# Two more pairs in the seven-product form, three decodings moved two stages on, two pieces of products moved

## The chip, the cores and the metric

The kernel runs on one core of one Trainium2 chip. The metric is device time in microseconds (us) of the whole kernel, as the median of the runs made. A profile of one execution comes with it: for every engine (TensorE = PE, VectorE = DVE, ScalarE = ACT, GpSimd = POOL, SyncE = SP, which issues the DMAs) it has the start and the duration of each instruction.

## The reference, cut to what matters

Linear attention with a decay, then a mixture of four experts, then one more gated network; all in fp32.

```python
x = retention(q, k, v, lam)              # 2 x 768 tokens, 8 heads of 64: x is 1536 x 512
p = domain_probs / (domain_probs.sum(-1, keepdims=True) + 1e-9)
out = 0
for e in range(4):                       # moe_w1: 4 x 512 x 1024, moe_w2: 4 x 1024 x 512
    out += p[:, e:e+1] * (relu(x @ w1[e]) @ w2[e])
h = out @ w_in                           # moe2_w_in: 512 x 2048
g = h * (1 / (1 + exp(-h)))
return g @ w_out                         # moe2_w_out: 2048 x 512
```

The two weights of the last network, moe2_w_in and moe2_w_out, come to the chip as 64-bit numbers and are brought to fp32 there.

## The kernel before, in words

The 1536 tokens are three groups of 512. Every fp32 product is made of three matmuls on fp32r halves: high x high, low x high, high x low. A high half is a copy by ACT, a low half a subtraction after it by DVE or POOL (`split`, lines 145 to 150).

There are four stages, one after the other on PE.

- **Stage a** (36 steps of `gemm1` and `gemm2`): attention for all tokens, and the experts for the first 512 tokens.
- **Stage c**: the experts for the other 1024 tokens. Each of 16 pairs `i` multiplies a 512 x 256 block of w1 by 1024 tokens in seven products instead of eight (`LEFT`, `product`, six matmuls each) and then multiplies the result by w2. Pairs 0 to 7 (`pair_step`) do that second multiplication plainly, as 8 pieces of 6 matmuls (`down`, line 803). Pairs 8 to 15 (`pair7`) do it by seven products for two pairs at a time, as 14 pieces of 6 matmuls (`down7`, line 981). `SW = NW // 2` is the first pair of the second kind.
- **Stage b**: the last network for the first 512 tokens, 16 steps of `gemm1` (12 matmuls, line 553) and, two steps later, `gemm2` (12 matmuls, line 609).
- **Stage d**: the last network for the other 1024 tokens, 8 pairs in `pair7`.

The order of the instructions on each engine is written out by hand. Between two products of a pair, `filler()` takes the next waiting piece from the list `fill`; `plan_n`, the last argument of `pair7`, says how many pieces come after each of the seven products. Each piece ends with an addition to the sum, put off to the next unit (`after`, `due`). In `pair7` the first product goes to a PSUM bank x, ACT copies x to y (line 1049), the second goes to z, and the third and fourth add to y, so that the third waits for the copy. After the fourth DVE makes v = y + s; from v, z, x and y come the gated values and their halves, in a chain over DVE and ACT.

In stage b, step `i` brings one 512 x 256 block of w_in in every second step: `left_sums` (four POOL sums, line 690) and `split_up` (one ACT copy, one POOL subtraction of 128x1024) for the block that PE uses two steps later. In the odd steps `split_down` does the same for w_out, and DMAs write three things for stage d to DRAM: the sums (`left_out`) and both halves of the block (`left_kept`). `combine` gives a list `mixing` of 11 jobs (differences on DVE, halves on ACT and DVE) that prepare the tokens for stage d; from step 3 on each step does one. Where a job has a second part, it is put in `pending` and is sent out at the start of the next step (`flush`).

A decoding (`decode`, 32 of them) takes 128x512 words of 64 bits to fp32: one ACT operation (line 200) and, after the next `flush`, four DVE operations (lines 207, 210, 213, 217; the last is the addition). `decode_next` stores the result of the decoding before, loads the words of a coming one and starts one. 18 of them are in stage a, 14 in pairs 0 to 6 of stage c.

Of the kernel before, what the change touches and what calls it, by code (L numbers as in the profile page):

```python
# [7 lines left out]
F32 = mybir.dt.float32  # L8
# [15 lines left out]
NF = 8  # L24
CW = B * P
TW = 512
HW = DM // 2
DECODE = 4
GI = 32
NN = 4  # L30
NW = E * NF // 2
NV = NF
SW = NW // 2


A12, A22, A21, A11 = range(4)
# [3 lines left out]
def kernel(  # L40
# [10 lines left out]
    nc = tc.nc  # L51
# [178 lines left out]
    def flush():  # L230
        while pending:
            pending.pop(0)()
# [475 lines left out]

    def left_kept(i):
        for n, t in enumerate(up_t["b", i]):  # L710
            nc.sync.dma_start(out=wu[i][:, n], in_=t[:, :4].bitcast(F32))

    def left_in(i):
        t = tmp["d"].tile([P, 4, HW], F32, tag="us", name="us")
# [435 lines left out]
    with tc.manual_schedule():  # L1150
# [75 lines left out]
        for i in range(NN, na):  # L1226
# [24 lines left out]
                load_gate("c", 0, 1)  # L1251
            if i == DECODE:
                start_decoder()
            elif DECODE < i < 4 * NF - NN and (i % 2 and i not in (5, 13) or i in (6, 14, 16, 18, 20, 22, 24, 26)):
                decode_next(i < 4 * NF - NN - 2)

            if i == NN:
                w_tiles(wp, ("a", 3))
# [19 lines left out]
                    job()  # L1278

        flush()  # L1280
        early.close()
        words.close()
        xa.close()
# [16 lines left out]
        for i in range(NW):  # L1300
# [29 lines left out]
                    jc.setdefault(gap, []).extend(lambda q=q: down_left(q) for q in qs)  # L1330
            if i == NW - 1:
                jc[4] = [lambda: split_up(("b", 0), False)]
            pair7(i - SW, jc, {SW: [1] * 7, SW + 1: [0, 1, 1, 1, 1, 1, 2]}.get(i))

        for _ in range(3):
            filler()
# [16 lines left out]
        for i in range(nb):  # L1353
            flush()
            gemm1("b", i)
            unit()
            if i < 2:
                for _ in range(3):
                    filler()
            elif i < nb - 2:  # L1360
                gemm2("b", i - 2)
            if i % 2:
                load(0)
                left_out(i // 2)
                for n in ([0, 1] if i == 1 else [i // 2 + 1]):
                    if n < NV:
                        left_kept(n)
                if i == nb - 3:
                    grp_t[("d", 0), 0] = hi, lo = up_tiles(wp)
                    split(nc.gpsimd, hi[:, 0], lo[:, 0], lead[0])  # L1370
                    split(nc.gpsimd, hi[:, 1:], lo[:, 1:], lead[1])
                if i < nb - 1:
                    split_down(("b", (i + 1) // 2))
                else:
                    fill += last_down("b", nb)
            else:
                left_sums(("b", i // 2))
                if i == nb - 2:
                    left_in2(0)
                if 2 <= i < nb - 2:  # L1380
                    split_up(("b", i // 2 + 1), False)
                if i == nb - 6:
                    lead = [
                        leftp.tile([P, 2 * DM], F32, tag="uc", name="lead")[:, :HW],
                        tmp["sums"].tile([P, 4, HW], F32, tag="lead", name="lead"),
                    ]
                    nc.sync.dma_start(out=lead[0], in_=wd[0][0][:, A11 * HW:])
                    nc.sync.dma_start(out=lead[1], in_=wu[0][:, 2])
            if i == 1:
                assert not fill  # L1390
                ops.close()
                tmp["sums"] = pool(sums, "sums2", side="right")
            if i == 2:
                mixing = combine(acc_t["c", 0], acc_t["c", 1])
            elif i > 2:
                for job in mixing[i - 3:i - 2]:
                    job()
        flush()
        sums.close()
        late.close()  # L1400
        tmp["d"] = tmp["s"] = tmp["op"] = pool(ctx, "dp", side="right")
# [2 lines left out]
        for i in range(NV):  # L1404
# [14 lines left out]
                plan.append((0, lambda: down_sums(i)))  # L1419
            for gap, fn in plan:  # L1420
                jobs.setdefault(gap, []).append(fn)
            pair7(i, jobs, {0: [0, 1, 1, 0, 1, 1, 1], 1: [0, 0, 1, 0, 0, 1, 2]}.get(i))
        for n, when in ((4, 0), (3, 0), (2, 3), (1, 5)):
            after(when, lambda n=n: down_left(7 * NV // 2 - n))
        fill[-1:] = [
# [61 lines left out]
```

## The time and the profile before

| what | value |
|---|---|
| median of 3 runs | 786.24 us (785.4 to 786.46) |
| the profiled execution's own time | 786.24 us |
| its span, from the first to the last instruction | 784.5 us |
| PE busy | 777.6 us, 99% of the span |
| DVE, ACT, POOL busy | 558.4, 370.3, 496.8 us |
| granted clock of TensorE | 1.00 of full speed all through |

The span is what the profile can explain; 1.7 us lie around it. Starts are in us from the start of the span. Busy time of PE includes the time in which a matmul's end is still on its way through the array, so that a busy PE can still lose time between the starts of two matmuls.

### The profile page before, as it was taken

The page shows a single profiled execution, that of the slowest core. Times are in us where ns is not written, and L with a number is a line of the kernel's source. Part 1 is how long each engine was busy: PE and PEld are TensorE (multiplying, and loading weights), DVE is VectorE, ACT ScalarE, POOL GpSimd, SP SyncE. Part 2 cuts the span into 40 slices and gives each one's busy share as a digit, 9 for nine tenths or more (in the row PEclk, how much of TensorE's full clock was granted, in tenths as well). Part 3 has the DMA queues.
Part 4 walks back from the last instruction along what each step waited for, and adds up shares of the span by engine and source line. Part 5 has one row for each costly group of instructions (what it writes and reads, how often), then busy time and mean ns, then how long its engine had stood idle before and what let it go on. Part 6 is the DMA issues. An engine that isn't in the chain of part 4 may idle for free.

```text
span 784.5 us, 11076 instructions
## 1 busy us (share of the span) xinstructions
PE 777.6 (99%) x4038; PEld 644.4 (82%) x4038; DVE 558.4 (71%) x812; ACT 370.3 (47%) x664; POOL 496.8 (63%) x458
## 2 busy tenths in 40 slices
PE   9999999999999999999999999999999999999998
PEld 8888888888888888888788888888888778888886
DVE  7345587786687588888778777784555577777775
ACT  3333434343455334433464646463445476666651
POOL 3856565443765455556698888877688855665642
PEclk9999999999999999999999999999999999999999
DMA  7877768553244334433102120215767525232302
GB/s 295 309 244 241 224 205 301 185 189 120 95 141 141 113 130 162 134 108 115 46 28 81 54 82 28 80 42 201 279 225 260 195 68 180 78 131 77 112 1 108
DMA packets 39913, 113.89 MB, mean 145 GB/s; under 512 B 4482, under 2 KB 6706, under 8 KB 39858
## 3 DMA queue, kind: packets, MB, share of 16 engines
q1 hardware_dynamic: 39856, 113.18, 42.6%
q8 instruction: 32, 0.52, 0.3%
q14 instruction: 23, 0.19, 0.1%
q10 hardware_dynamic: 2, 0.00, 0.0%
HBM read 89.02 MB, written 24.14 MB: 144 GB/s over the span
## 4 chain that ended last, share of the span: by engine, by line
PE 83%; DVE 12%; ACT 3%; issue 2%; ACTq 0%; DVEq 0%
PE po L981 19%; PE po L609 17%; PE ph L553 16%; PE y L755 10%; PE x L755 6%; PE z L755 6%; PE po L803 4%; DVE acc L817 3%; PE s L419 2%; ACT hhi L782 2%; PE xps L458 2%; DVE hlo L785 1%; DVE dec L213 1%; DVE dec L217 1%; DVE dec L207 1%
## 5 line engine op out<-in xcount | busy, mean ns | idle before, releaser
L150 POOL TENSOR_TENSOR ub<-u,ua 128x1024 fp32r<-128x1024 f32 (+2 forms) x41 | 70.2, 1712 | 105.0 <-ACT ua L149 92.3
L150 POOL TENSOR_TENSOR dl<-d,dh 128x1024 fp32r<-128x1024 f32 (+1 forms) x33 | 79.3, 2403 | 24.9 <-ACT dh L149 24.8
L150 POOL TENSOR_TENSOR ub<-us,ua 128x1024 fp32r<-128x1024 f32 x23 | 56.0, 2436 | 28.8 <-ACT ua L149 28.8
L579 ACT ACTIVATE hhi<-ph 128x512 fp32r<-128x512 f32 x40 | 24.0, 599 | 103.7 <-DVE ph L573 85.1
L609 PE MATMUL po<-hhi,dh 128*128 128x512 f32 (+1 forms) x208 | 57.2, 379 | 0.0
L609 PE MATMUL po<-hhi,dl 128*128 128x512 f32 (+1 forms) x208 | 55.9, 373 | 0.0
L609 PE MATMUL po<-hlo,dh 128*128 128x512 f32 (+1 forms) x208 | 55.9, 372 | 0.0
L553 PE MATMUL ph<-xhi,ua 128*128 128x512 f32 (+1 forms) x208 | 53.3, 378 | 0.8 <-ACT xhi L474 0.8
L553 PE MATMUL ph<-xhi,ub 128*128 128x512 f32 (+1 forms) x208 | 52.2, 373 | 0.0
L553 PE MATMUL ph<-xlo,ua 128*128 128x512 f32 (+1 forms) x208 | 52.1, 372 | 0.0
L803 PE MATMUL po<-hhi,dh 128*128 128x512 f32 x128 | 49.8, 389 | 0.0
L803 PE MATMUL po<-hhi,dl 128*128 128x512 f32 x128 | 49.8, 389 | 0.0
L803 PE MATMUL po<-hlo,dh 128*128 128x512 f32 x128 | 49.8, 389 | 0.0
L946 DVE TENSOR_TENSOR acc<-po,acc 128x512 f32<-128x512 f32 x56 | 38.0, 685 | 14.7 <-PE po L981 14.7
L580 DVE TENSOR_TENSOR hlo<-ph,hhi 128x512 fp32r<-128x512 f32 x40 | 27.7, 692 | 27.4 <-ACT hhi L579 27.4
L946 DVE TENSOR_TENSOR a<-po,a 128x512 f32<-128x512 f32 (+1 forms) x50 | 33.6, 676 | 18.0 <-PE po L981 17.6
L817 DVE TENSOR_TENSOR acc<-po,acc 128x512 f32<-128x512 f32 x56 | 36.9, 681 | 10.5 <-PE po L803 10.5
L149 ACT ACTIVATE dh<-d 128x1024 fp32r<-128x1024 f32 (+2 forms) x52 | 40.2, 796 | 7.8 <-issue 2.9
L553 PEld LDWEIGHTS ph<-xhi,ua 128*128 128x128 f32 x208 | 36.8, 188 | 8.5 <-ACT xhi L474 1.0
L609 PEld LDWEIGHTS po<-hhi,dl 128*128 128x128 f32 x208 | 37.8, 188 | 7.1
L609 PEld LDWEIGHTS po<-hlo,dh 128*128 128x128 f32 x208 | 37.8, 188 | 7.0
L609 PEld LDWEIGHTS po<-hhi,dh 128*128 128x128 f32 x208 | 37.1, 188 | 7.5 <-ACT hhi L579 0.2
(214 smaller groups left out, 2165.2 us busy)
## 6 DMA issues: line engine op xcount, KB each, us to landing
u<-wts SPq DMA_DIRECT2D x32, 512.0 KB, 3.5
d<-wts SPq DMA_DIRECT2D x32, 512.0 KB, 4.0
words<-wts SPq DMA_DIRECT2D x32, 512.0 KB, 4.7
wd<-dec SPq DMA_DIRECT2D x32, 256.0 KB, 3.0
d<-wd SPq DMA_DIRECT2D x16, 512.0 KB, 4.0
qkt<-qk SPq DMA_DIRECT2D x12, 512.0 KB, 4.6
kvt<-kv SPq DMA_DIRECT2D x10, 512.0 KB, 4.4
u<-wd SPq DMA_DIRECT2D x8, 512.0 KB, 4.1
```

Source lines behind the costliest of these rows:

```text
L149: nc.scalar.activation(out=hi, in_=src, func=AF.Copy)
L150: eng.tensor_tensor(out=lo, in0=src, in1=hi.bitcast(F32), op=ALU.subtract)
L419: nc.tensor.matmul(s[t, p // n][:, p % n], lhsT=qkt[r, 1, p], rhs=qkt[r, 0, p], start=True, stop=True,)
L553: nc.tensor.matmul(pt[:, :n], lhsT=w, rhs=x[:, k, o:o + n], start=(j == 0), stop=(j == len(ops) - 1),)
L579: nc.scalar.activation(out=hi, in_=pt, func=AF.Copy)
L580: nc.vector.tensor_tensor(out=lo, in0=pt, in1=hi.bitcast(F32), op=ALU.subtract)
L609: nc.tensor.matmul(po_t[d][:, o:o + n], lhsT=w[:, d * P:(d + 1) * P], rhs=h[:, :n], start=(begin and j == 0), stop=(last and j == 2), skip ...
L755: nc.tensor.matmul(to, lhsT=a[:, k * P:(k + 1) * P], rhs=b[:, k], start=(first and j == 0), stop=(j == len(ops) - 1), skip_group_check=not ...
L803: nc.tensor.matmul(po, lhsT=w, rhs=h, start=(j == 0), stop=(j == len(ops) - 1))
L817: nc.vector.tensor_tensor(out=a, in0=po, in1=a, op=ALU.add)
L946: eng.tensor_tensor(out=out, in0=a, in1=b, op=op)
L981: nc.tensor.matmul(po[:, part], lhsT=w, rhs=h[:, part], start=(fresh and j == 0), stop=(j == len(ops) - 1), skip_group_check=not fresh,)
```

## The change

`SW` becomes 6: pairs 6 and 7 of stage c are done in the seven-product form too. Stage c then has only 10 decodings. Stage a gets one more, at its step 28; stage b gets three, at its steps 5, 6 and 7, with a pool and a first loading of words at step 1. The `mixing` jobs leave those three steps and are put two to a step at steps 8, 10 and 12. In the first seven-product pair of stage c, one piece moves from behind the sixth product to behind the second. In the first pair of stage d, one moves from behind the fifth product to behind the first. `left_kept` no longer writes the quarter A21 of a block, and writes the rest with two DMAs instead of one.

```diff
--- before.py
+++ after.py
@@ -26,11 +26,13 @@
 TW = 512
 HW = DM // 2
 DECODE = 4
+A_JOBS = (6, 7, 9, 11, *range(14, 29))
+B_JOBS = (5, 6, 7)
 GI = 32
 NN = 4
 NW = E * NF // 2
 NV = NF
-SW = NW // 2
+SW = 6
 
 
 A12, A22, A21, A11 = range(4)
@@ -708,7 +710,8 @@
 
     def left_kept(i):
         for n, t in enumerate(up_t["b", i]):
-            nc.sync.dma_start(out=wu[i][:, n], in_=t[:, :4].bitcast(F32))
+            for part in (slice(A12, A22 + 1), slice(A11, A11 + 1)):
+                nc.sync.dma_start(out=wu[i][:, n, part], in_=t[:, part].bitcast(F32))
 
     def left_in(i):
         t = tmp["d"].tile([P, 4, HW], F32, tag="us", name="us")
@@ -1251,8 +1254,8 @@
                 load_gate("c", 0, 1)
             if i == DECODE:
                 start_decoder()
-            elif DECODE < i < 4 * NF - NN and (i % 2 and i not in (5, 13) or i in (6, 14, 16, 18, 20, 22, 24, 26)):
-                decode_next(i < 4 * NF - NN - 2)
+            elif i in A_JOBS:
+                decode_next(i < A_JOBS[-2])
 
             if i == NN:
                 w_tiles(wp, ("a", 3))
@@ -1278,6 +1281,7 @@
                     job()
 
         flush()
+        store_decoded()
         early.close()
         words.close()
         xa.close()
@@ -1330,7 +1334,7 @@
                     jc.setdefault(gap, []).extend(lambda q=q: down_left(q) for q in qs)
             if i == NW - 1:
                 jc[4] = [lambda: split_up(("b", 0), False)]
-            pair7(i - SW, jc, {SW: [1] * 7, SW + 1: [0, 1, 1, 1, 1, 1, 2]}.get(i))
+            pair7(i - SW, jc, {SW: [1, 2, 1, 1, 1, 0, 1], SW + 1: [0, 1, 1, 1, 1, 1, 2]}.get(i))
 
         for _ in range(3):
             filler()
@@ -1354,6 +1358,10 @@
             flush()
             gemm1("b", i)
             unit()
+            if i in B_JOBS:
+                decode_next(True)
+            elif i == B_JOBS[-1] + 1:
+                store_decoded()
             if i < 2:
                 for _ in range(3):
                     filler()
@@ -1386,16 +1394,23 @@
                     ]
                     nc.sync.dma_start(out=lead[0], in_=wd[0][0][:, A11 * HW:])
                     nc.sync.dma_start(out=lead[1], in_=wu[0][:, 2])
-            if i == 1:
+            if i == B_JOBS[-1] + 2:
+                assert jobs[0] == 4 * NV
+                words.close()
+            elif i == 1:
                 assert not fill
                 ops.close()
+                words = ExitStack()
+                dec["pool"] = pool(words, "decb")
+                start_decoder()
                 tmp["sums"] = pool(sums, "sums2", side="right")
             if i == 2:
                 mixing = combine(acc_t["c", 0], acc_t["c", 1])
-            elif i > 2:
-                for job in mixing[i - 3:i - 2]:
-                    job()
+            else:
+                for _ in range({3: 1, 4: 1, 8: 2, 9: 1, 10: 2, 11: 1, 12: 2, 13: 1}.get(i, 0)):
+                    mixing.pop(0)()
         flush()
+        assert not mixing
         sums.close()
         late.close()
         tmp["d"] = tmp["s"] = tmp["op"] = pool(ctx, "dp", side="right")
@@ -1419,7 +1434,7 @@
                 plan.append((0, lambda: down_sums(i)))
             for gap, fn in plan:
                 jobs.setdefault(gap, []).append(fn)
-            pair7(i, jobs, {0: [0, 1, 1, 0, 1, 1, 1], 1: [0, 0, 1, 0, 0, 1, 2]}.get(i))
+            pair7(i, jobs, {0: [1, 1, 1, 0, 0, 1, 1], 1: [0, 0, 1, 0, 0, 1, 2]}.get(i))
         for n, when in ((4, 0), (3, 0), (2, 3), (1, 5)):
             after(when, lambda n=n: down_left(7 * NV // 2 - n))
         fill[-1:] = [
```

## Rows read from the trace of the kernel before

**Rows 1.** The page: the span, and PE's busy time, share and instructions.

```profile
span 784.5 us, 11076 instructions
...
PE 777.6 (99%) x4038; PEld 644.4 (82%) x4038; DVE 558.4 (71%) x812; ACT 370.3 (47%) x664; POOL 496.8 (63%) x458
```

**Rows 2.** PE's waits, the one for a copy to y: total, times, longest.

```profile
PE y L755 <- ACT y L1049: 0.7, 2, 0.4
```

**Rows 3.** Windows: pair 6 before (plain form), then pair 10 (seven-product form).

```profile
349.72:370.12 20.40, 20.40 (x92) 16.89 (x90) 17.50 (x27) 8.40 (x14) 13.46 (x10) 1.00 0.28 85
...
408.78:427.82 19.04, 19.04 (x85) 15.77 (x84) 14.76 (x24) 9.73 (x22) 15.48 (x19) 1.00 0.24 83
```

**Rows 4.** Timeline of PE in stage c's first seven-product pair (start, duration).

```profile
375.33 0.39 PE L803 MATMUL po<-hlo,dh 128*128 128x512 f32 x1
376.01 0.73 PE L755 MATMUL y<-hi,ua 128*128 128x512 f32 x2 [0.29 <-ACT y L1049]
...
393.82 0.62 PE L755 MATMUL y<-hi,ua 128*128 128x512 f32 x2
```

**Rows 5.** Timeline of ACT there: the two copies for PE's third product.

```profile
375.37 0.59 ACT L1049 ACTIVATE y<-x 128x512 f32<-128x512 f32 x1
...
392.36 0.58 ACT L1049 ACTIVATE y<-x 128x512 f32<-128x512 f32 x1
```

**Rows 6.** Timeline of DVE late in stage a: one decoding, then the next.

```profile
171.88 0.42 DVE L207 TENSOR_SCALAR dec<-words 128x512 uint32<-128x512 uint32 x1
...
172.55 0.69 DVE L213 SCALAR_TENSOR_TENSOR dec<-words,dec 128x512 uint32<-128x512 uint32 x1
173.27 0.69 DVE L217 CUSTOM_DVE_ANT_0 dec<-dec,tail 128x1024 uint16<-128x1024 uint16 x1
173.88 2.63 DVE L207 TENSOR_SCALAR dec<-words 128x512 uint32<-128x512 uint32 x1
...
188.08 0.70 DVE L573 SCALAR_TENSOR_TENSOR ph<-ph,gate 128x512 f32<-128x512 f32 x1 [2.57 <-PE ph L553]
```

**Rows 7.** Timeline of POOL: late in stage a, then in stage b.

```profile
173.79 2.44 POOL L150 TENSOR_TENSOR ub<-u,ua 128x1024 fp32r<-128x1024 f32 x1 [7.70 <-ACT ua L149]
...
568.07 3.09 POOL L150 TENSOR_TENSOR dl<-d,dh 128x1024 fp32r<-128x1024 f32 x1 [3.35 <-ACT dh L149]
571.12 0.73 POOL L690 TENSOR_TENSOR us<-u 128x256 f32<-128x256 f32 x1
...
584.08 2.41 POOL L150 TENSOR_TENSOR ub<-u,ua 128x1024 fp32r<-128x1024 f32 x1
```

**Rows 8.** Timeline of DVE in stage b: a difference, then step 6's multiplication.

```profile
567.69 1.22 DVE L656 TENSOR_TENSOR sum<-acc,sum 128x1024 f32<-128x1024 f32 x1
...
570.15 0.70 DVE L586 TENSOR_TENSOR ph<-ph,gate 128x512 f32<-128x512 f32 x1 [1.25 <-ACT gate L585]
```

**Rows 9.** Timeline of ACT: a decoding's operation in stage a, a split's copy in b.

```profile
172.09 0.68 ACT L200 ACTIVATE words<-words 128x512 f32<-128x512 f32 x1
...
582.26 1.05 ACT L149 ACTIVATE ua<-u 128x1024 fp32r<-128x1024 f32 x1
```

**Rows 10.** Timeline of PE in stage b: step 10's first and second four matmuls.

```profile
588.30 1.07 PE L553 MATMUL ph<-xhi,ua 128*128 128x512 f32 x4
589.21 1.07 PE L553 MATMUL ph<-xhi,ub 128*128 128x512 f32 x4
```

**Rows 11.** Timeline of PE in stage d: third product of the first and second pair.

```profile
620.12 0.73 PE L755 MATMUL y<-hi,ua 128*128 128x512 f32 x2 [0.37 <-ACT y L1049]
...
635.31 0.73 PE L755 MATMUL y<-hi,ua 128*128 128x512 f32 x2
```

**Rows 12.** Timeline of ACT and DVE in stage d's first pair: y's copy, v.

```profile
619.47 0.59 ACT L1049 ACTIVATE y<-x 128x512 f32<-128x512 f32 x1
...
624.59 0.70 DVE L946 TENSOR_TENSOR v<-y,s 128x512 f32<-128x512 f32 x1 [4.28 <-DMA wu<-us]
```

**Rows 13.** The line of `left_out` in stage b: its DMAs' time from issue to landing.

```profile
DMA to landing us min/median/max: 5.0/5.1/6.5
```

## The prediction

> **What bounds the kernel now.** I read the page first, then PE's waits, windows of single pairs, and the timelines of PE, ACT, DVE and POOL around the places that the change touches. PE is busy for 777.6 of 784.5 us [rows 1], and its waits hold little: all that it waits for copies to y is 0.7 us in two places [rows 2]. Busy time can hide a late start, so the measure is the distance between starts. A plain pair takes 20.40 us for 90 matmuls, a seven-product pair 19.04 us for 84 [rows 3]; both are 0.2267 us a matmul. In starts more than 0.26 us apart after the attention there are four losses only: 0.45 us in stage c's first seven-product pair (375.33 to 376.01, where 0.23 was due) [rows 4], 0.54 us before the third product of stage d [rows 11], 0.10 us in d's second pair, and 0.76 us just after. So the time follows the number of matmuls, and whatever makes PE wait comes on top. DVE, ACT and POOL cost nothing until something that they make is late for PE.
>
> **Matmuls removed.** Pairs 6 and 7 go from 90 to 84 matmuls each: 12 x 0.2267 = 2.72 us less. PE has no gap there to lose them in. The weights' extra sums on POOL are what the pairs after them do already inside 19.04 us [rows 3]. This term I take as sure.
>
> **A piece moved in stage c.** The third product now waits for ACT's copy to y, which starts at 375.37 and ends at 375.96 [rows 5]. Its queue is held up by the pair before, and that pair will look the same two pairs earlier. With one more piece ahead, the product is due 1.36 us later than its 375.56, so the wait goes: -0.45 us. The piece is missing behind the sixth product, and there the chain over v, z and x ends in the next pair's copy to y, now done at 392.94 for a product at 393.82 [rows 4, 5], 0.88 us early. That product comes 0.58 us nearer to the pair's start (0.45 for the wait gone, 0.13 for the slower first matmul behind a wait), while the chain starts 0.8 us later and loses one addition of 0.6 us; I get some 0.1 us to spare. Bounds: no loss, or 0.5 us, the removed wait given back. I take none.
>
> **Decodings.** Four fewer in stage c free DVE and ACT where PE was not waiting for them: nothing. One more in stage a: uncontended, its four DVE operations go from 171.88 to 173.96, 2.08 us [rows 6]. It falls after 183 us, and before 188.08 DVE sits idle for 2.57 us [rows 6]; what is made there is used two steps, 10.9 us, later. Nothing; without that idle time it would still be 2 us against 5 or more. The store added at the stage's end has long been free to go.
>
> The three in stage b are the heart of it. The rows show DVE and POOL excluding each other where both read SBUF. A decoding's first operation, 0.42 us alone, took 2.63 at 173.88: it ended 0.28 us after POOL's subtraction, which ran from 173.79 to 176.23 [rows 6, 7]. It goes the other way too: DVE's difference ended at 568.91 [rows 8] and POOL's subtraction, sent at 568.07, only then began, and took 2.25 us to 571.16 [rows 7]. So an operation that had to wait takes 0.14 us less than its time alone after the other has ended (DVE 0.28 and 0.55, POOL 2.25 and 0.6), and they take turns. The Trainium skill says the same in "SBUF — State Buffer", Who interferes with whom: the pair of ports that the two share is an exclusive lock, and the loser blocks fully. By that rule, with which the trace agrees, a decoding is no longer 2.08 us hidden under PE but port time added to POOL's; without it the sum would lack the next term and stand at case N below.
>
> In steps 5 to 8 I followed the port by hand. As now, DVE is free at 567.7, and step 6 starts on PE at 566.54 (each step is 24 x 0.2267 = 5.44 us, counted back from 588.30 [rows 10]). ACT does the decoding's 0.68 us [rows 9] ahead of the copy for `split_down`, so POOL asks at 568.6 and gets the port at 569.05.
>
> Port, from 569.05: down weights 2.25 to 571.30; the last operation of the first decoding to 571.85, so that step 6's multiplication comes at 571.8 instead of 570.15 [rows 8]; four left sums (0.73 each, 0.6 after a wait [rows 7]) with two operations of the second decoding between, to 575.0; the low half of the up weights to 577.26; two more operations to 578.44. Then the port is idle for 1.9 us: the next down copy on ACT stands behind step 7's high half and the third decoding, which stand behind DVE. Three operations of that decoding end at 581.7; down weights to 583.95; its last operation to 584.5. Only then comes step 8's multiplication, and behind it on ACT the high half and at 585.65 the copy of the up weights for step 10, 582.26 before [rows 9]. On the port: three left sums to 586.5; step 8's difference (one of its two mixing jobs) to 587.57; the fourth sum to 588.17; the low half from the other job to 589.25; the low half of the up weights, 2.25 us, to 591.50.
>
> Before, that subtraction started at 584.08 and ended at 586.49 [rows 7], and step 10's second four matmuls read it at 589.21 [rows 10]: 2.7 us of room. Five us later it is 2.3 us late, and PE waits: **+2.3 us**. Bounds: nothing, if the port's turns fall better (the two mixing operations alone are 2.1 us of it), and 3.3 us if each waiting operation takes its full time. The other consumers have room: step 8's earlier block is due at 578.33 and done at 577.26; the lower halves of steps 6 to 8 are due 5 us or more after they are made. Later, at steps 10 to 13, the doubled mixing jobs have port time to spare once PE itself is 2.3 us later.
>
> **Stage d's first pair.** y's copy ends at 620.06 and PE's product starts at 620.12 [rows 11, 12], 4.62 us after the pair's start at 615.50. With a piece moved ahead it is due at 5.44. Mixing's end in stage b comes some 1.2 us later on DVE (two low halves in a row before step 13's multiplication), but if PE has lost 2.3 us the copy is at about 4.7: no wait. That takes away 0.54 us. It is not a gain. From v on, DVE and ACT are a chain: v starts at 624.59 [rows 12] and the second pair's third product, the first thing that needs its end, starts 10.72 us later, at 635.31 [rows 11]. v is made from the fourth product, which follows the third by a piece: from the third's due start at 5.44 come three times six matmuls (4.08), and v follows the last by 0.26 (as now: 620.12, 0.11 for the slower first matmul, 4.08, and 624.59 is 0.28 later), so v starts at 9.78 from the pair's start, instead of 9.09. The chain's end moves by the same **+0.69 us**: the room that a piece gives ahead of the third product is taken from behind the fourth. Bounds: 0.69, or 1.15 if y's copy itself comes late (case N).
>
> **`left_kept`.** 16 more DMA issues, a quarter fewer bytes. SP waits for nothing that PE needs there; at 0.37 us an issue it is 0.75 us more in each odd step. Nothing, with the exception that is a rival below.
>
> **Sum** (the profiled execution's own time is 786.24, which is also the median of the runs): 786.24 - 2.72 - 0.45 + 2.3 + 0.69 = 786.06, say **786.0 us**, -0.03%.
>
> **Rivals.** A measurement of this kernel tells about 0.2% (1.57 us) from no change.
>
> Case N, the decodings stay hidden: the port's turns fall so that the up weights of step 10 come by 589.2. For it: of the 22.45 us from 569.05 to 591.50 the port is idle for 1.9, and the two mixing operations (2.15) may fall behind that subtraction instead of ahead of it; together that is more than the 2.3 us. Against it: every one of the turns that I followed has its pattern in the trace. Then d's copy ends about 5.8 us after the pair's start, v starts 0.11 + 4.08 + 0.26 later, at 10.24, and the last term is 1.15: 786.24 - 2.72 - 0.45 + 1.15 = 784.2. Chance 0.30.
>
> Case S, slower: the sums of step 8 on POOL can't start until `left_out` of step 7 has left their buffer. SP sends it behind the store of the second decoding, which stands behind that decoding's end at 578.44; so it goes at 579.3 instead of 574.5 and lands 5.1 us later, at most 6.5 [rows 13], at 584.4 to 585.8, against POOL free at 584.5. With more traffic (0.5 MB of words and 0.25 MB of store a decoding) it lands later, and past 584.5 each us goes nearly whole into PE's wait at step 10. From a landing about 7.4 us after the issue on, PE's wait is over 4.1 us and the change is slower: 788.1. Against it: the words are all loaded by step 6, and `left_kept` writes less. Chance 0.14.
>
> The forecast, a wait of 1.2 to 3.3 us at step 10, has 0.56; its own range is 784.9 to 787.1, for waits of 1.2 and 3.3 us; with scatter, 0.06 of its chance lies on the faster side of 0.2% (784.67). That gives faster 0.36, same 0.50, slower 0.14. The range over the cases, from N with 0.4 us of scatter to just short of S, is 783.8 to 787.8.
>
> **What the profile after would show.** Pairs 6 and 7 at 19.04 us; no start over 0.26 us apart at the third product of c's first seven-product pair; step 10 of stage b with a gap before its fifth matmul, ended by POOL's subtraction for the up weights, and four decoding lines there with means well over 0.42 and 0.69; the wait before d's third product gone and one of some 1.3 us at the second pair's. The prediction is wrong if step 10 has no gap (then 784.2), or if a gap appears in pair 7 or at steps 8 or 12 of stage b, where I have 0.1 to 1.1 us of room.

## The result, and the profile after

The changed kernel takes 789.8 us (median of 4 runs, 789.13 to 791.16) against 786.18 us for the kernel before on the same chip: a ratio of 1.0051 [1.0039, 1.0063]. It is slower, by 3.6 us. The prediction was 786.0 us, with 783.8 to 787.8 as its range: it was wrong, and the time moved the way to which it had given a chance of 0.14. (The three decodings that the title calls moved two stages on went from stage c to stage b, which follows it on PE.)

The profiled execution took 789.13 us, with a span of 787.0 us and a granted clock of 1.00 throughout. First the page and PE's waits by releaser (total, times, longest).

```profile
span 787.0 us, 11130 instructions
...
PE 775.9 (99%) x4026; PEld 641.9 (82%) x4026; DVE 569.6 (72%) x822; ACT 376.0 (48%) x684; POOL 513.5 (65%) x480
```

```profile
PE ph L555 <- POOL ub L152: 2.8, 2, 1.9
PE y L758 <- ACT y L1052: 1.4, 2, 1.3
...
PE y L758 <- ACT s L770: 1.0, 1, 1.0
...
PE y L758 <- ACT s L1022: 0.2, 1, 0.2
```

PE has 12 matmuls fewer and 1.7 us less busy time [rows 1], yet the span is 2.5 us longer. As in the prediction, the busy share hides it; the starts show it. The windows of pairs 6 and 7, the two that changed form:

```profile
330.48:349.52 19.04, 19.04 (x85) 15.77 (x84) 13.53 (x21) 6.97 (x12) 9.92 (x10) 1.00 0.14 51
349.52:369.13 19.61, 19.43 (x85) 15.62 (x84) 16.27 (x27) 11.74 (x25) 19.30 (x24) 1.00 0.14 41
```

Pair 6 takes the 19.04 us that were forecast [rows 3]; pair 7 takes 0.57 more. Where else PE starts late, read from PE's timeline after the attention as the distance between two starts less the 0.227 us of a matmul:

| place | before | after | released by |
|---|---|---|---|
| stage c's first pair | 0 | 1.17 | ACT's copy to s |
| first seven-product pair | 0.45 | 0 | |
| second seven-product pair | 0 | 0.35 | ACT's copy to s |
| stage b, step 6 | 0 | 1.06 | POOL's subtraction |
| stage b, step 10 | 0 | 2.10 | POOL's subtraction |
| stage d, first and second pair | 0.54 + 0.10 | 0.31 + 1.46 | ACT's copy to y |
| stage d, behind that | 0.76 | 0.76 | ACT's addition |
| sum | 1.85 | 7.21 | |

That is 5.36 us more waiting, less 2.72 us of matmuls: +2.64, against 2.5 us between the spans. That the two agree so well is in part luck. The sum leaves out the slower first matmul behind each wait (0.11 us, and there are three waits more), and from the end of the attention to the start of its last matmul PE takes 3.25 us longer; but the attention ends 0.15 us earlier, and behind PE's last start the span has 3.39 us left instead of 3.99. Now the rows of the three waits that the prediction does not have, and of the largest. PE's timeline at these four places (start, duration; the idle time before it and its releaser at the end):

```profile
224.26 0.73 PE L758 MATMUL y<-hi,ua 128*128 128x512 f32 x2 [1.01 <-ACT s L770]
...
356.74 0.73 PE L758 MATMUL y<-hi,ua 128*128 128x512 f32 x2 [0.18 <-ACT s L1022]
...
566.94 1.19 PE L555 MATMUL ph<-xhi,ub 128*128 128x512 f32 x4 [0.90 <-POOL ub L152]
...
590.94 1.21 PE L555 MATMUL ph<-xhi,ub 128*128 128x512 f32 x4 [1.94 <-POOL ub L152]
```

SP's timeline, its DMA issues, at the end of stage a and at step 3 of stage b:

```profile
218.43 0.33 SPq L121 DMA_DIRECT2D u<-wts  x1
218.85 0.38 SPq L227 DMA_DIRECT2D wd<-dec  x1
...
549.45 0.86 SPq L239 DMA_DIRECT2D words<-wts  x2
550.40 0.38 SPq L121 DMA_DIRECT2D u<-wd  x1
551.18 0.71 SPq L709 DMA_DIRECT2D wu<-us  x1
```

ACT's timeline in stage c's first pair, and around the second seven-product pair:

```profile
223.12 0.60 ACT L770 ACTIVATE s<-z 128x512 f32<-128x512 f32 x1 [3.70 <-DMA wd<-dec]
...
352.88 0.58 ACT L1052 ACTIVATE y<-x 128x512 f32<-128x512 f32 x1
...
356.08 0.60 ACT L1022 ACTIVATE s<-y 128x512 f32<-128x512 f32 x1
```

POOL's timeline in stage b: the first sum and the subtraction for step 6, then what it does for step 10:

```profile
560.71 0.74 POOL L692 TENSOR_TENSOR us<-u 128x256 f32<-128x256 f32 x1 [2.84 <-DMA wu<-us]
...
564.49 2.39 POOL L152 TENSOR_TENSOR ub<-u,ua 128x1024 fp32r<-128x1024 f32 x1
...
580.31 2.67 POOL L152 TENSOR_TENSOR dl<-d,dh 128x1024 fp32r<-128x1024 f32 x1 [3.37 <-ACT dh L151]
583.65 0.73 POOL L692 TENSOR_TENSOR us<-u 128x256 f32<-128x256 f32 x1 [0.67 <-DMA wu<-us]
...
587.55 3.34 POOL L152 TENSOR_TENSOR ub<-u,ua 128x1024 fp32r<-128x1024 f32 x1
```

**Stage c's first pair.** The store of stage a's last decoding is issued at 218.85, and ACT's copy to s waits until it has left its buffer: the pool of `s` takes over that memory. **Step 6.** The words for stage b, two loads of 0.5 MB, are issued at 549.45, just ahead of `left_out` of step 3 at 551.18. POOL's first sum then waits 2.84 us for that transfer, 9.5 us after its issue; four sums and a subtraction later PE is 1.06 us late. Before, `left_out` was issued at 551.88 and the sum found its buffer free at 559.40. **Step 10.** The subtraction for the up weights ends at 590.89; the prediction had 591.50. DVE's timeline shows who had the port before it:

```profile
580.76 2.76 DVE L219 CUSTOM_DVE_ANT_0 dec<-dec,tail 128x1024 uint16<-128x1024 uint16 x1
...
585.41 1.57 DVE L658 TENSOR_TENSOR sum<-acc,sum 128x1024 f32<-128x1024 f32 x1
586.91 1.76 DVE L651 TENSOR_TENSOR lo<-sum,hi 128x1024 fp32r<-128x1024 f32 x1
```

The turns came in the order of the prediction: the third decoding's last operation ends at 583.52 (584.5 was forecast), step 8's difference at 586.98 (587.57), the low half at 588.67 (589.25), and only then does the subtraction get through. DVE's decoding operations in stage b, grouped by line and shape (behind the bar, the busy time in us and the mean in ns):

```profile
L219 DVE CUSTOM_DVE_ANT_0 dec<-dec,tail 128x1024 uint16<-128x1024 uint16 x3 | 6.6, 2215 | 0.1
L212 DVE TENSOR_SCALAR tail<-words 128x512 uint32<-128x512 uint32 x3 | 3.5, 1152 | 0.0
L209 DVE TENSOR_SCALAR dec<-words 128x512 uint32<-128x512 uint32 x3 | 2.9, 960 | 0.0
```

A decoding's first operation (L209 here) took 0.42 us alone and its last (L219) 0.69 [rows 6]. Here one operation after another had to sit out a POOL subtraction: L209 took 2.05 us at 565.12, L212 2.62 at 567.09, and L219 2.77 at 574.72 and 2.76 at 580.76; the first two ended 0.29 us after that subtraction, the other two 0.55 and 0.54. The Trainium skill states the rule behind it in "SBUF — State Buffer", Who interferes with whom (the pair of ports is an exclusive lock, and the loser blocks fully); these four durations agree with it.

### The profile page after: what moved, and what is told of

It is laid out like the page before. It is cut to its first block, busy times and chain, and to the rows that moved or that the text cites. A ratio compares the mean times of both kernels' runs of the same rounds, so it can differ in the third digit from the quotient of the medians.

```text
span 787.0 us, 11130 instructions
## 1 busy us (share of the span) xinstructions
PE 775.9 (99%) x4026; PEld 641.9 (82%) x4026; DVE 569.6 (72%) x822; ACT 376.0 (48%) x684; POOL 513.5 (65%) x480
## 4 chain that ended last, share of the span: by engine, by line
PE 83%; DVE 5%; POOL 4%; issue 4%; ACT 2%; DMA 2%; SPq 0%; DVEq 0%; ACTq 0%; POOLq 0%
PE po L984 22%; PE y L758 12%; PE ph L555 11%; PE po L611 10%; PE po L806 8%; PE z L758 7%; PE x L758 7%; PE s L421 2%; POOL ub L152 2%; POOL dl L152 2%; PE xps L460 1%; PE xps L456 1%; POOL us L692 1%; DMA wu<-ub 1%; DVE olo L944 1%
## 5 line engine op out<-in xcount | busy, mean ns | idle before, releaser
L152 POOL TENSOR_TENSOR dl<-d,dh 128x1024 fp32r<-128x1024 f32 (+1 forms) x31 | 75.6, 2439 | 14.8 <-ACT dh L151 14.7
L949 DVE TENSOR_TENSOR acc<-po,acc 128x512 f32<-128x512 f32 x70 | 47.5, 685 | 19.1 <-PE po L984 19.1
L555 PEld LDWEIGHTS ph<-xhi,ub 128*128 128x128 f32 x208 | 37.2, 188 | 10.6 <-POOL ub L152 3.7
L692 POOL TENSOR_TENSOR us<-u 128x256 f32<-128x256 f32 x48 | 40.7, 848 | 5.0 <-DMA wu<-us 5.0
L942 ACT ACTIVATE ohi<-v 128x512 fp32r<-128x512 f32 x30 | 18.0, 600 | 52.8 <-DVE v L1038 27.6
L555 PEld LDWEIGHTS ph<-xlo,ua 128*128 128x128 f32 x208 | 37.3, 188 | 7.0
```

The costliest lines, as they stand in the source:

```text
L152: eng.tensor_tensor(out=lo, in0=src, in1=hi.bitcast(F32), op=ALU.subtract)
L555: nc.tensor.matmul(pt[:, :n], lhsT=w, rhs=x[:, k, o:o + n], start=(j == 0), stop=(j == len(ops) - 1),)
L692: nc.gpsimd.tensor_tensor(out=s[:, n], in0=a, in1=b, op=op)
L942: nc.scalar.activation(out=hi, in_=src, func=AF.Copy)
L949: eng.tensor_tensor(out=out, in0=a, in1=b, op=op)
```

## The experiments

Each is an edit of the changed kernel unless it says otherwise; times are medians, ratios are to the kernel before on the same chip, whose median lay between 785.89 and 786.18 us. What is said of waits is read from one profiled execution of each version.

### The store at stage a's end: store_early

```diff
+            elif i == A_JOBS[-1] + 2:
+                store_decoded()
             elif i in A_JOBS:
...
         flush()
-        store_decoded()
         early.close()
```

> The changed kernel, with the store of stage a's last decoding sent at step 30 instead of after the stage. Theory of the late store: in the changed kernel it goes out at 218.85 us, behind SP's loads, and ACT's copy to s in c's first pair (223.1) waits until it has landed, since s lies where the decoding's tiles were; PE loses 1.17 us there. Sent at step 30, it is long done: no start of PE over 0.26 us apart in c's first pair, about 1.2 us less than the changed kernel's 789.1 (profile 785.8 span). Rival, that the copy is late because DVE and POOL still work off the decoding of step 28: the wait stays, and the time with it.

788.15 us (10 runs), 1.0023 [1.0013, 1.0033]. PE's timeline in stage c's first pair has no wait:

```profile
222.38 0.61 PE L611 MATMUL po<-hlo,dh 128*128 128x512 f32 x2
222.83 0.62 PE L758 MATMUL y<-hi,ua 128*128 128x512 f32 x2
```

So 1.17 us of the loss is that store's place in the queue, and has nothing to do with how many products a pair has. The edit stands in most of the versions below.

### The split of `left_kept`: kept_whole

```diff
-            for part in (slice(A12, A22 + 1), slice(A11, A11 + 1)):
-                nc.sync.dma_start(out=wu[i][:, n, part], in_=t[:, part].bitcast(F32))
+            nc.sync.dma_start(out=wu[i][:, n], in_=t[:, :4].bitcast(F32))
```

> The changed kernel, with left_kept as before (whole halves, one DMA each). It tells who delays the landing of left_out of step 3, for which POOL's sums of step 4 wait until 560.71 us, so that step 6's second four matmuls start 1.06 us late. Theory of the split DMAs: twice the issues, in small rows, hold up SP and the DMA engines; with whole halves the landing is back near 5.1 us after its issue and the wait at step 6 is gone (1.1 us less). Rival, the words: 1 MB of them is loaded just ahead; then the landing stays at 8 us or so and the wait stays. By either, step 10's wait of 2.1 us stays within 0.5.

790.14 us, 1.0047 [1.0032, 1.0062], against 1.0051 [1.0039, 1.0063] for the change: these runs tell no difference that the split makes. The wait at step 6 is there with whole blocks too, 2.03 us, and after it the clock fell (below); step 10, which PE reaches that much later, is then late by 0.59 us only.

### Where the words are loaded: words_later

With `store_early`'s edit:

```diff
                 dec["pool"] = pool(words, "decb")
-                start_decoder()
...
+            if i == 3:
+                start_decoder()
```

> The changed kernel with the early store of stage a's last decoding, and the first two loads of words in stage b sent at the end of step 3 instead of step 1. In the run with the early store alone, POOL's sums of step 4 still waited 1.16 us for the landing of left_out of step 3 (some 7.8 us after its issue; 6.5 in the kernel before), and in other runs of the change step 6 waited 1 to 2 us for what comes after those sums. Theory of the words: the 1 MB ahead of left_out on SP's queue makes it late; sent behind it, left_out lands 5 to 6.5 us after its issue, the sums of step 4 wait under 0.3 us and no run waits at step 6; the slowest of the runs with the clock under 1.0 become rarer. Step 10's 2 us stay. Rival: DMA traffic of step 1 itself (halves of two blocks); then the landing stays late.

788.23 us (6 runs), 1.0031 [1.0018, 1.0043]: no gain over 788.15. The wait at step 6 does come from the words: in all seven traces in which they stand ahead of `left_out`, POOL's first sum waits for that DMA (1.16 us in `store_early`, 2.84 after, 3.65 in `kept_whole`); here it does not, and in the traces without words there it waits 0.33 us at most. POOL's timeline, DVE's and PE's:

```profile
555.87 0.74 POOL L692 TENSOR_TENSOR us<-u 128x256 f32<-128x256 f32 x1
...
585.10 3.33 POOL L152 TENSOR_TENSOR ub<-u,ua 128x1024 fp32r<-128x1024 f32 x1
```

```profile
559.00 3.28 DVE L651 TENSOR_TENSOR lo<-acc,hi 128x1024 fp32r<-128x1024 f32 x1 [1.20 <-ACT hi L650]
```

```profile
588.48 1.20 PE L555 MATMUL ph<-xhi,ub 128*128 128x512 f32 x4 [2.65 <-POOL ub L152]
```

But step 10 lost 2.81 us, against 1.97 in the profile of `store_early` and 2.10 after. After, PE was held at step 6 and so came to step 10 later. In `store_early` it was not held (the sum's 1.16 us fell inside the room), and the difference to it lies on the port: the subtraction for step 6, which no longer stands behind a late sum, starts at 558.79 here, just ahead of a low half on DVE, which then takes 3.28 us instead of 1.40. DVE's multiplications of steps 5 to 8 come 0.54 to 0.65 us later, step 10's subtraction ends 0.47 later, and PE comes to it 0.37 earlier. So what was gained at step 6 can be given back at step 10.

### The port alone: b_one_op

With `store_early`'s edit:

```diff
+            if job >= 4 * NV - len(B_JOBS):
+                dec["out"] = (wd[i][j, :, n * DM:(n + 1) * DM], f)
+                return
             tail = decp.tile([P, DM], U32, tag="tail", name="tail")
```

> The changed kernel with the early store, and of the three decodings in stage b only ACT's operation and the first of the four DVE operations: three are left out, so the last quarter of the last block of weights isn't decoded. Words are loaded and results stored as before. Theory of the port: without the nine operations the up weights' subtraction for step 10 ends at 586 to 588 us on the run's own time, and PE's wait of 2 us at step 10 goes (under 0.3). Rival, the queue of SP: left_out of step 7 stands behind the store of the second decoding, POOL's sums wait for its landing; the store is still there, so 1 us or more of wait stays.

It leaves out nine of the twelve operations that DVE has for the three decodings. 785.7 us (10 runs), 1.0 [0.9989, 1.0011]: 2.45 us under `store_early` (1.8 by the two ratios), with the same loads, stores, ACT operations and mixing. In the profiled execution step 10 does not wait, PE's timeline:

```profile
588.08 1.07 PE L558 MATMUL ph<-xhi,ua 128*128 128x512 f32 x4
588.98 1.07 PE L558 MATMUL ph<-xhi,ub 128*128 128x512 f32 x4
```

PE had lost 1.96 us at step 6 there, and some 1.6 us to the clock (below), but that gave step 10 no room: DVE's multiplications now wait for PE, by way of ACT's gate, so that the chain moves with PE. DVE's timeline at step 8:

```profile
580.81 0.70 DVE L591 TENSOR_TENSOR ph<-ph,gate 128x512 f32<-128x512 f32 x1 [3.05 <-ACT gate L590]
```

After, that multiplication came right behind the decoding's last operation. SP's queue is not excluded by this run alone, since the decodings' stores go out earlier in it too. The trace after excludes it: POOL's wait of 0.67 us for `left_out` of step 7 ends at 583.65, and until 583.52 the port was DVE's anyway. So step 10 is late by DVE's operations on the port that it shares with POOL.

### The mixing jobs' place: mix_as_before

```diff
-            else:
-                for _ in range({3: 1, 4: 1, 8: 2, 9: 1, 10: 2, 11: 1, 12: 2, 13: 1}.get(i, 0)):
+            elif i > 2:
+                for job in mixing[:1]:
                     mixing.pop(0)()
```

> The changed kernel, with one mixing job a step from step 3 on, as before, and the decodings of stage b as changed. Theory of the port: mixing and decoding share it; steps 5 to 7 now hold both, so the up weights' subtractions for steps 8 and 10 come later still: PE waits there 2 to 5 us in all (2.1 at step 10 in the changed kernel). Rival, that the two mixing jobs at step 8 cause step 10's wait: it shrinks below 1 us. In d's first pair y's copy is 1 us earlier against PE by either.

794.44 us, 1.0105 [1.009, 1.012]: 4.6 us more than the change (4.2 by the ratios). PE's waits:

```profile
PE ph L555 <- POOL ub L152: 3.1, 3, 1.2
PE ph L555 <- ACT ua L151: 2.4, 1, 2.4
```

PE is late at steps 6, 8 and 10, by 0.96, 1.25 and 2.57 us and then 1.42 more. With the decodings in steps 5 to 7, moving the jobs out of them was a needed part of the change. In stage d y's copy comes 2.48 us after the pair's start here, and the third product does not wait.

### No decodings in stage b: no_b_decode

```diff
-A_JOBS = (6, 7, 9, 11, *range(14, 29))
+A_JOBS = (6, 7, *range(9, 29))
...
-            if i in B_JOBS:
-                decode_next(True)
-            elif i == B_JOBS[-1] + 1:
-                store_decoded()
```

> The changed kernel, with the three decodings of stage b (and its loading of words) done in stage a at steps 10, 12 and 13 instead. All else, the mixing jobs' order too, as in the changed kernel. Theory of the port: the decodings' port time is what makes step 10 of stage b late; without them the up weights' subtraction for step 10 ends by 587.5 and PE's 2.1 us there are gone. The words' theory says that step 6's 1.06 us go too. Then stage b loses nothing and the time is 3 us or more under the changed kernel's, about 786 with the store's wait still in it. Rival, the mixing jobs, two at step 8: without decodings step 10 still waits 1 us or more. Stage a may lose something at steps 10 to 14: none is expected, up to 1 us.

791.91 us, 1.0075 [1.0058, 1.0092]. Stage b has no late start at all, steps 6 and 10 included, while stage d loses the same 0.31 and 1.46 us as after. But stage a pays for the three more: DVE's timeline, then PE's.

```profile
85.41 2.72 DVE L219 CUSTOM_DVE_ANT_0 dec<-dec,tail 128x1024 uint16<-128x1024 uint16 x1
88.05 2.47 DVE L634 TENSOR_TENSOR acc<-po,gate 128x512 f32<-128x512 f32 x4
```

```profile
88.78 0.50 PE L611 MATMUL po<-hhi,dh 128*128 128x512 f32 x1 [4.58 <-DVE acc L634]
...
89.44 0.63 PE L611 MATMUL po<-hlo,dh 128*128 128x512 f32 x1
89.87 0.63 PE L611 MATMUL po<-hhi,dh 128*128 128x512 f32 x1
```

A decoding stands ahead of the additions that free a PSUM bank, and its last operation takes 2.72 us behind a POOL subtraction.

### The pieces: d_plan_back and c_plan_back

```diff
-{0: [1, 1, 1, 0, 0, 1, 1], 1: [0, 0, 1, 0, 0, 1, 2]}
+{0: [0, 1, 1, 0, 1, 1, 1], 1: [0, 0, 1, 0, 0, 1, 2]}
```

> The changed kernel with stage d's first pair as before (the moved piece back behind the fifth product). My step: the piece only moves the wait, since v's chain is of fixed length. The changed kernel waits 0.31 us at the third product and 1.46 at the second pair's. Back: the wait at the third product is 1.4 to 1.8 us, that of the second pair 0.1, so the sum is within 0.3 us of 1.77. Rival, that the move brings something: the sum is 0.7 us or more larger.

788.96 us in one run. PE is late by 1.66 and 0.10 us in stage d's two pairs instead of 0.31 and 1.46: 1.76 against 1.77. The moved piece only moves the wait.

```diff
-{SW: [1, 2, 1, 1, 1, 0, 1], SW + 1: [0, 1, 1, 1, 1, 1, 2]}
+{SW: [1] * 7, SW + 1: [0, 1, 1, 1, 1, 1, 2]}
```

> The changed kernel with one edit: c's first seven-product pair has its pieces as before, one behind each product. Theory (the moved piece takes 0.45 us there and gives back 0.35 in the next pair, where ACT's copy of s comes late): the wait of 0.45 us before the third product of the first such pair is back, and the start 0.57 us apart in the next pair is gone; the sum is 0.1 us more. Rival (the next pair's wait comes from the extra sums of pairs 6 and 7 or from a fuller queue of ACT, not from the moved piece): both waits stand, and the sum is 0.45 us more. All else as in the changed kernel (789.1 to 790 us).

790.56 us in one run (it lost more in stage b: 1.55 us at step 6, 2.40 at step 10, and the clock fell behind that). In stage c it is as the first theory had it: 0.45 us at the third product of the first seven-product pair is back, and the second has no late start. PE's timeline:

```profile
335.67 0.50 PE L758 MATMUL y<-hi,ua 128*128 128x512 f32 x1 [0.29 <-ACT y L1052]
...
356.21 0.62 PE L758 MATMUL y<-hi,ua 128*128 128x512 f32 x2
```

### The two pairs without the decodings: seven_only

Three decodings are left out (which, its expectation says); the store is early, and stage b, `left_kept` and stage d are as before.

```diff
             nc.sync.dma_start(out=to, in_=f.bitcast(F32))
+            for job in range(29, 32) if jobs[0] == 29 else ():
+                i, j, n = job // 4, job // 2 % 2, job % 2
+                nc.sync.dma_start(out=wd[i][j, :, n * DM:(n + 1) * DM], in_=f.bitcast(F32))
```

> Leaves three of the 32 decodings out: the last one that is made is stored in the places of the other three, so that the three blocks hold wrong numbers but every later load and product is done. With the store of stage a's last decoding sent early, stage b, the kept halves and stage d as before, and c's moved piece. It sizes what the two pairs give when nothing is paid for decodings. Theory: 12 matmuls (2.72 us) and the 0.45 us of c's first seven-product pair, less the 0.35 us of the pair after it: 2.8 us less than the kernel before, 783.2 us, span 781.7, and PE's late starts only those of the next pair (0.35), and of stage d as before (0.54, 0.10, 0.76). Rival (the seven-product pairs themselves pay, since POOL makes the weights' extra sums there): late starts of 0.5 us or more in pairs 6 to 9, and 784 us or more.

783.23 us (4 runs), 0.9963 [0.995, 0.9977], span 781.6; late starts 0.35, 0.53, 0.10 and 0.76 us, as expected. So the two pairs give 2.9 us (2.72 for the matmuls, and some 0.1 for the moved piece), and the rest is the price of the decodings' new places, of the mixing jobs that made way for them, and of the store.

### Other places for them: c_decodes, a31_c2, c2_b1

All three have the early store, `left_kept` and stage d as before, and stage c's moved piece.

```diff
-                if i == SW - 2:
+                if i in (0, 1, 2, SW - 2):
                     jc.setdefault(6, []).extend([flush, lambda: decode_next(True)])
```

> What is left of the change when its costs are avoided: seven products in pairs 6 to 15, stage c's moved piece, one more decoding in stage a with an early store; the other three decodings in pairs 0, 1 and 2 of stage c (behind the seventh product); stage b, left_kept and stage d's first pair as before. Theory: PE loses only the matmuls and the 0.1 us that the moved piece leaves (0.45 gone, 0.35 new in the next pair): 2.7 to 2.9 us under the kernel before, 783.2, a ratio of 0.9965. Rival: DVE is full in pairs 1 and 2 (17.5 of 20.4 us with two decodings, some 2.1 to 3.4 us more with three), so that a gate comes late for PE and 1 us or more is lost there: 784.2 to 786.

784.68 us (11 runs), 0.999 [0.998, 0.9999]: a little faster than the kernel before, and the best that keeps all the work. PE's waits show what the three cost in stage c, 1.32 us of late starts in the plain pairs:

```profile
PE z L757 <- DVE hlo L787: 0.3, 1, 0.3
PE po L805 <- POOL dl L152: 0.2, 1, 0.2
...
PE x L757 <- DVE hlo L787: 0.2, 1, 0.2
```

In `a31_c2` one of them moves to stage a's step 31, and pair 2 has none:

```diff
-A_JOBS = (6, 7, 9, 11, *range(14, 29))
+A_JOBS = (6, 7, 9, 11, *range(14, 29), 31)
...
-                if i in (0, 1, 2, SW - 2):
+                if i in (0, 1, SW - 2):
```

> As the version with three decodings in stage c (784.68 us, 0.999 of the kernel before), but one of the three goes to stage a's step 31, with its store two steps later; pairs 0 and 1 of stage c keep one each. Theory (a decoding costs what it delays on the port of DVE and POOL, wherever it stands; the 1.25 us of waits that c's pairs 3 and 5 show are the price of three decodings there): with one fewer in c the waits after pair 2 lose about a third or more of their 1.25 us, and stage a has room at step 31, so the span is 0.4 to 0.9 us shorter: 783.8 to 784.3 us. Rival (stage a is as tight at its end as stage b): a wait of 1 us or more appears between 200 and 224 us, and the time is 785.3 us or more.

785.58 us (11 runs), 0.9995 [0.9986, 1.0004]. The rival came true: stage c's loss shrinks to 0.05 us, but the end of stage a loses 2.04, in PE's timeline:

```profile
216.13 0.73 PE L757 MATMUL x<-hi,ua 128*128 128x512 f32 x2 [1.14 <-ACT ua L151]
...
220.28 0.73 PE L757 MATMUL z<-hi,ub 128*128 128x512 f32 x2 [0.33 <-POOL ub L152]
```

In `c2_b1` that one goes to stage b instead, alone, with its words loaded late (as in `words_later`):

```diff
-B_JOBS = (5, 6, 7)
+B_JOBS = (6,)
...
-                for _ in range({3: 1, 4: 1, 8: 2, 9: 1, 10: 2, 11: 1, 12: 2, 13: 1}.get(i, 0)):
+                for _ in range({6: 0, 12: 2, 14: 0, 15: 0}.get(i, 1) if i > 2 else 0):
```

> The two pairs in the seven-product form, the store of stage a's last decoding early, kept halves and stage d as before; of the three decodings two in pairs 0 and 1 of stage c (they cost 0.05 us of late starts where a third decoding went to stage a), and one in stage b, at step 6, its words loaded after step 3; one mixing job goes from step 6 to step 12. Theory (the port holds one more decoding in stage b: its 2.1 us, spread over an odd step, against the 2.7 us of room that step 10's subtraction had in the kernel before, and the words come too late to hold back the kept sums of step 3): no late start at steps 6 to 12 of stage b, late starts as with the decodings left out plus 0.05, so a span of 781.7 us and 783.3 us, 1.4 us under the version with three in stage c (784.68). Rival (stage b has no room for even one, its turns on the port already being taken): a wait of 0.5 to 2 us at step 8, 10 or 12, and 784 to 785.5 us.

785.78 us (11 runs), 0.9997 [0.9988, 1.0006]. My theory fell. PE's timeline at step 10 and in stage d's first pair:

```profile
587.72 0.96 PE L555 MATMUL ph<-xhi,ub 128*128 128x512 f32 x3 [0.86 <-POOL ub L152]
...
619.90 0.72 PE L757 MATMUL y<-hi,ua 128*128 128x512 f32 x2 [1.50 <-ACT y L1051]
```

One decoding already makes step 10 late by 1.02 us, and one mixing job put to step 12 makes stage d's first pair late by 1.66, 1.12 more than before. Stage b had no room for even this one.

## Why the prediction was wrong

**Matmuls removed: right.** Pair 6 takes 19.04 us, and `seven_only` measures the whole at 2.9 us with the piece.

**The port at step 10: right.** +2.3 was forecast, 2.10 measured, in the place and by the instruction named, and the port's last turns came in the order forecast; `b_one_op` removes it. Case N, with 0.30, did not come. That the number is so close is partly luck: with PE held at step 6 or not, the other traces with all three decodings in stage b and the mixing jobs moved have 0.59 to 2.81 us there. The turns on the port that [rows 6, 7] showed in stage a carried over to stage b.

**The store at stage a's end: the largest error.** The step that failed is "The store added at the stage's end has long been free to go." Its data was ready, but it was issued at 218.85, behind the block's load, and I never asked who takes its source buffer over. ACT's copy to s does, 4 us later. Nothing was forecast and 1.17 us measured; `store_early` takes it away.

**Traffic in stage b: not priced.** Under `left_kept` I wrote "SP waits for nothing that PE needs there", and case S looked at `left_out` of step 7 only, because "the words are all loaded by step 6". The same mechanism, a kept sum that lands late, struck three steps earlier, while the first two blocks of words load: 1.06 us at step 6. For `left_out` of step 7, where I had put it, POOL waited 0.67 us. Its cause is shown by `words_later`; what it costs on its own is not settled, since step 10 can take back what step 6 gives: at both together PE lost 3.16 us after, 2.81 in `words_later` and 1.97 in `store_early`.

**The piece in stage c: half right.** The 0.45 us went. "I get some 0.1 us to spare" held for the copy to y that I followed (353.60 is on time), but ACT's next copy, to s at 356.08, did not have it: 0.35 us back. My bound of 0.5 held it; the value that I took was nothing. That gap in pair 7 is one of the signs of being wrong that the prediction had named. `c_plan_back` shows that the two belong together: the piece is worth 0.1 us.

**Stage d: the mechanism right, the size off.** +0.69 was forecast, (0.31 + 1.46) - (0.54 + 0.10) = 1.13 measured. The step that failed is "if PE has lost 2.3 us the copy is at about 4.7": it started 5.10 us after the pair's start (622.51 less 617.41), so what PE lost at step 10 did not bring it nearer. The loss is the 1.15 of case N. In `no_b_decode`, where stage b has no decoding and loses nothing, the copy starts 5.11 us after the pair's start all the same; in `c2_b1`, with a single moved job and the old order of pieces, it is 5.10, and the loss 1.12 more than before; in `mix_as_before`, with no doubled job, 2.48. So it is the doubled mixing job of step 12, and the moved piece does not mend it (`d_plan_back`).

The errors in the profiled execution: 1.17 + 1.06 + 0.35 + 0.44, less 0.2 at step 10, is 2.8 us; the sum of the terms had been -0.18, and +2.64 came, counted in the same way. The rest of the way to 789.8 is not in that span: 0.4 us more lie around it (2.13 us against 1.74), which no run here explains, and the median is 0.7 us above the profiled execution, whose clock was 1.00, while two of the four runs had a mean granted clock of 0.998 and spans of 788.2 and 789.0. What lies behind those is the last section.

The range was too narrow because it held the bounds of the terms that I had and nothing for a transfer that becomes late in a place that I had not followed.

## What to carry to other kernels

A cut in TensorE's work was worth its matmuls here (2.72 of the 2.9 us that came with all else free); what decided was where the displaced work went. A decoding, 2.08 us of DVE, cost 2.04 us of waiting at stage a's end, 1.02 in stage b (and 1.12 for the job that made way for it), 1.27 as the third in stage c, where two cost 0.05: price such a job, place by place, against the room of the tightest consumer on the engine that shares its port, not against busy shares. For every added DMA ask two things beyond whether its data is ready: what stands behind it in its queue, and who gets its source buffer next.

## What the runs showed of the hardware that was not expected

**The clock falls after some waits.** In `kept_whole` PE waited 2.03 us at step 6; about 1.5 us after it started again, the granted clock was at half, the lower of its two levels (1.2 GHz instead of 2.4), for 3.3 us. Windows of `kept_whole` (length, PE busy, weight loads, DVE, ACT, POOL, then the granted clock, the DMA share and GB/s):

```profile
560.00:565.00 5.00, 5.00 (x24) 4.14 (x23) 2.60 (x3) 3.36 (x5) 3.45 (x4) 1.00 0.67 270
569.40:572.70 3.30, 3.30 (x9) 2.56 (x8) 2.78 (x3) 1.05 (x2) 2.60 (x3) 0.50 1.07 417
573.00:578.00 5.00, 5.00 (x23) 4.13 (x22) 4.97 (x5) 1.96 (x3) 4.13 (x4) 1.00 0.33 120
```

Eight matmuls' weight loads in 3.3 us instead of some 15: starts are 0.427 us apart, not 0.227, and about 1.6 us are lost beyond the wait itself. The same is seen after the 4.58 us wait in `no_b_decode` (the starts at 89.44 and 89.87 above), in `b_one_op`, `mix_as_before` and `c_plan_back`, with 1.5 to 1.6 us each. It does not follow every wait: after 2.65 us in `words_later` four matmuls took 1.20 us, while in `c_plan_back`, after 2.24 us at the same place, they took 2.07:

```profile
591.08 2.07 PE L555 MATMUL ph<-xhi,ub 128*128 128x512 f32 x4 [2.24 <-POOL ub L152]
```

So a wait here could cost some 1.6 us more than its length. What decides it was not settled. Some 3.3 us at half clock make a mean of 0.998 over 788 us, which is what the two longer runs of the change have; but those runs have no trace.

**A transfer of 0.5 MB behind two loads of words of 0.5 MB each** held its buffer for 9.5 us from issue to POOL's next start (551.18 to 560.71), where its line had landed in 5.0 to 6.5 us before [rows 13].
